# A routed feed-forward kernel: the second layer's third tile in Strassen's form on two column halves

## The chip, the core and the metric

The kernel runs on one core of one Trainium2 chip. The metric is the device time of one execution in microseconds. The core's engines run side by side, each from its own instruction queue: TensorE (PE in the profile, its weight loads PEld) multiplies matrices, VectorE (DVE) and ScalarE (ACT) work element by element, GpSimd (POOL) does so too and here also issues the indirect transfers (gathers and scatters), SyncE (SP) issues plain transfers.

## What is computed

Attention with a decay, block by block, then a layer that sends each token to one of eight experts:

```python
for b in range(nb):                         # 12 blocks of 64 positions, 4 batches, 8 heads of 64
    intra = einsum('bhic,bhjc->bhij', qb, kb) * Dmask
    out[:, :, sl] = einsum('bhij,bhjd->bhid', intra, vb) + einsum('bhid,bhde->bhie', qb * lam_pow, kv_state)
    kv_state = lam_block * kv_state + einsum('bhsd,bhse->bhde', kb * rev_pow, vb)

logits = x @ w_gate                         # x: 3072 tokens of 512
expert_idx = argmax(logits, axis=1)
gate_w = probs[arange(N), expert_idx]       # softmax of the logits
for e in range(8):
    h = maximum(x[mask] @ w1[e], 0.0)       # 512 -> 1024
    out[mask] = gate_w[mask, None] * (h @ w2[e])   # 1024 -> 512
```

All of it is in fp32.

## The kernel before

Everything is written for a scheduler that works from priorities: the program's order gives each instruction its rank, the pools give buffers, and the scheduler fixes one order for each engine's queue and puts in the semaphores. An engine then takes its own queue strictly in that order. Some instructions are pinned to the written order (`keep_in_program_order`).

The attention comes first (to about 125 us in the profile). It leaves every token's row in a table in memory (`xs`) and writes each token into a list of its expert. After it come nine passes over the experts. Passes `0a` and `0b` are the first expert in two parts, multiplied in the plain way (`hidden`, `outputs`). The other seven experts are sorted by their number of tokens, and each is one pass with 424, 408, 408, 384, 368, 368 and 360 places (the "fast" passes). A pass has tiles of 128 places; with 424 or 408 places there is a fourth one of 40 or 24.

Each fast pass multiplies with Strassen's method in Winograd's form. A product of two by two blocks is built from seven products instead of eight, of sums of the blocks of the left side (s1 to s4) and of the right (t1 to t4). `form` (L481) gives the seven products and their additions, `left_sums` (L495) and `right_sums` (L502) the sums before them.

- First layer, `hidden_fast` (L540): the left side is the first weight matrix, its sums made by GpSimd (`first_sums`, tiles `s_q`, `s_k`, `s_v`, and one in place in `w1t`), the right side the tokens, turned so that features lie on the partitions (`xgT`), their sums by VectorE (`token_sums`). The loop runs over two chunks of four of the eight feature chunks: seven products a chunk, each of four matmuls (L549) of 128x128 weights by half the places. Products take three PSUM banks in turn (`ph_banks`); a product can begin once the product three before it has been read out by VectorE or ScalarE. The sums land in `hT`, and ScalarE applies the relu (L560).
- Second layer, `outputs_fast` (L570): `pair_sums` (L562) has VectorE make the sums of tiles 0 and 1 of `hT` in four operations of 512 columns (tiles `h_qsT`, `h_qT`, `h_kT`, `h_kd`). Then tile 2, and tile 3 where there is one, are multiplied in the plain way by `outputs` (L596): eight matmuls (L608) of a tile's `hT` by 512 columns of the second weights `w2t`. A tile of at most 64 (or 32) places is spread over two (or four) groups of the array's columns, with the eight matmuls taking the groups in turn, and the partial results are added afterwards. Then the pair of tiles 0 and 1 by `form` (seven products of four matmuls, L577, 128x128 by 256), with sums of `w2t` that GpSimd made (`second_sums`, tiles `t_q`, `t_k`, `t_v`, `t_m`). Each result is multiplied by the token's gate and scattered to its row (L440). Products take banks 7, 4 and 5 in turn.
- Between them, for the next pass: `turn` (L458) transposes the gathered rows (L463) into two PSUM banks, from which VectorE and ScalarE copy them into `xgT` (L450, L448). `fetch` (L426) gathers the rows of the pass after that; it waits until the transposes have released the gather's buffer.

GpSimd's sums are one instruction of 1024 columns each (L510, L513), eight a pass. The sums of the first weights and those of the second share three tags of one pool (`q`, `k`, `v`, three buffers each), so each waits for an earlier one's last reader.

The order of a fast pass on TensorE, as it is in the profile: first layer; transposes of the next pass, with one matmul of tile 2 (two records) between their two halves; the rest of tile 2; tile 3; the pair. The last pass has no transposes.

Of the kernel before, what the change touches and what calls it, by code (L numbers as in the profile page):

```python
# [10 lines left out]
F32 = mybir.dt.float32  # L11
I32 = mybir.dt.int32
AX = mybir.AxisListType
ALU = mybir.AluOpType
ACT = mybir.ActivationFunctionType
# [5 lines left out]
def kernel(  # L21
# [459 lines left out]
    def form(product, sums_of, temps, give):  # L481

        a, b = sums_of
        p1, u2, u3, u4 = temps
        nc.scalar.copy(p1, product(a.a11, b.b11))
        nc.vector.tensor_add(u2, product(a.s2, b.t2), p1)
        nc.vector.tensor_add(u3, product(a.s3, b.t3), u2)
        p5 = product(a.s1, b.t1)
        give(1, 1, p5, u3)
        nc.vector.tensor_add(u4, p5, u2)  # L490
        give(0, 0, product(a.a12, b.b21), p1)
        give(0, 1, product(a.s4, b.b22), u4)
        give(1, 0, product(a.a22, b.t4), u3)

    def left_sums(a, s1, s2, s3, s4, sub, add):  # L495
        sub(s3, a[0][0], a[1][0])  # L496
        add(s1, a[1][0], a[1][1])
        sub(s2, s1, a[0][0])
        sub(s4, a[0][1], s2)
        return SimpleNamespace(a11=a[0][0], a12=a[0][1], a22=a[1][1], s1=s1, s2=s2, s3=s3, s4=s4)  # L500

    def right_sums(b, t1, t2, t3, t4, sub):  # L502
# [3 lines left out]
        sub(t4, b[1][0], t2)  # L506
        return SimpleNamespace(b11=b[0][0], b21=b[1][0], b22=b[1][1], t1=t1, t2=t2, t3=t3, t4=t4)

    def pool_add(o, x, y):
        return nc.gpsimd.tensor_tensor(out=o, in0=x, in1=y, op=ALU.add)  # L510

    def pool_sub(o, x, y):
        return nc.gpsimd.tensor_tensor(out=o, in0=x, in1=y, op=ALU.subtract)  # L513

    def pool_sub_last(o, x, y):

        tc.keep_in_program_order(pool_sub(o, x, y))

    def first_sums(w1t):
        a = [[w1t[:, j * DH:(j + 1) * DH, i * FH:(i + 1) * FH] for j in range(2)] for i in range(2)]  # L520
# [17 lines left out]
        m.b = right_sums(b, t1, t2, b[0][1], t4, nc.vector.tensor_sub)  # L538

    def hidden_fast(m, w):  # L540
        m.hT = ffn.tile([P, FC, m.n], F32, tag="hT", name="hT", bufs=1)
        h = m.n // 2

        for c in range(0, FC // 2, 2):
            def product(lhs, rhs):
                p = bank(next(ph_banks), [P, 2, h], "p")
                for i in range(2):
                    for dc in range(DH):
                        nc.tensor.matmul(p[:, i, :], lhsT=lhs[:, dc, (c + i) * P:(c + i + 1) * P],  # L549
                                         rhs=rhs[:, dc, :], start=(dc == 0), stop=(dc == DH - 1))  # L550
                return p

            outs = [[m.hT[:, i * FC // 2 + c:i * FC // 2 + c + 2, k * h:(k + 1) * h]
                     for k in range(2)] for i in range(2)]
            temps = [work.tile([P, 2, h], F32, tag=t, name=f"u_{t}", bufs=n)
                     for t, n in (("qT", 2), ("kT", 2), ("qsT", 4), ("kd", 2))]
            form(product, (w, m.b), temps,
                 lambda i, k, p, u: nc.vector.tensor_add(outs[i][k], p, u))  # L558
            for i, k in ((1, 1), (0, 0), (0, 1), (1, 0)):
                nc.scalar.activation(outs[i][k], outs[i][k], ACT.Relu)  # L560

    def pair_sums(m):  # L562

        a = [[m.hT[:, j * FC // 2:(j + 1) * FC // 2, i * P:(i + 1) * P] for j in range(2)]
             for i in range(2)]
        sums = [work.tile([P, FC // 2, P], F32, tag=t, name=f"h_{t}", bufs=n)
                for t, n in (("qT", 2), ("kT", 2), ("qsT", 4), ("kd", 2))]
        return left_sums(a, *sums, nc.vector.tensor_sub, nc.vector.tensor_add)

    def outputs_fast(m, w2t, w2):  # L570
        a = pair_sums(m)
        outputs(m, w2t, range(2, len(m.widths)))

        def product(lhs, rhs):
            p = bank(next(po_banks), [P, MD // 2], "p")
            for fc in range(FC // 2):
                nc.tensor.matmul(p, lhsT=lhs[:, fc, :], rhs=rhs[:, fc, :],  # L577
                                 start=(fc == 0), stop=(fc == FC // 2 - 1))
            return p

        o = [ffn.tile([P, MD], F32, tag="o", name="o", bufs=4) for i in range(2)]
        outs = [[o[i][:, k * MD // 2:(k + 1) * MD // 2] for k in range(2)] for i in range(2)]
        two = [work.tile([P, 2, MD // 2], F32, tag="x", name="u", bufs=3) for i in range(2)]
        temps = [two[i][:, k, :] for i in range(2) for k in range(2)]

        def give(i, k, p, u):
            gate = at(m, i)[2]
            nc.scalar.activation(outs[i][k], u, ACT.Copy, scale=gate)
            nc.vector.scalar_tensor_tensor(out=outs[i][k], in0=p, scalar=gate, in1=outs[i][k],  # L589
                                           op0=ALU.mult, op1=ALU.add)  # L590

        form(product, (a, w2), temps, give)
        for i in range(2):
            scatter(at(m, i)[1], o[i])

    def outputs(m, w2t, tiles=None):  # L596
        for t in tiles or range(len(m.widths)):
            w = m.widths[t]


# [250 lines left out]
```

## Time and profile before

Fourteen runs took 471.04 to 475.26 us, the median is 472.95 us. One execution was profiled: it took 472.61 us, and its span from the first to the last instruction is 470.8 us. Engines are counted busy by their instructions; matmuls are pipelined and their ends are modelled, so their rows overlap, and the steps between the starts say how long one holds the array.

| stretch of the profiled execution (us) | length | PE busy | DVE busy | ACT busy | POOL busy |
|---|---|---|---|---|---|
| 161.4 to 182.0, pass 0b | 20.60 | 20.60 | 6.06 | 3.38 | 12.06 |
| 182.0 to 227.7, pass with 424 places | 45.70 | 45.70 | 20.07 | 9.93 | 38.09 |
| 227.7 to 270.7, 408 | 43.00 | 43.00 | 19.60 | 9.10 | 25.59 |
| 270.7 to 312.5, 408 | 41.80 | 41.80 | 19.39 | 9.06 | 25.58 |
| 312.5 to 351.0, 384 | 38.50 | 38.50 | 16.68 | 8.20 | 24.44 |
| 351.0 to 388.9, 368 | 37.90 | 37.90 | 16.47 | 8.09 | 25.31 |
| 388.9 to 427.9, 368 | 39.00 | 37.91 | 20.70 | 8.12 | 20.21 |
| 427.9 to 470.8, 360 and the end | 42.90 | 36.02 | 14.30 | 7.13 | 4.11 |
| whole execution: 472.61 us, span | 470.8 | 452.3 | 222.4 | 125.8 | 247.7 |

A row of the profile gives an instruction's line, its engine, what it writes from what (out<-in), the shapes, how long it took, and, in brackets, how long its engine stood idle before it and what ended that wait. An fp32 matmul leaves two records on PE and two weight loads on PEld.

### The profile page before, as it was taken

How to read it: one execution, taken by the hardware profiler on the slowest of the kernel's cores; microseconds unless marked ns; L12 is line 12 of the kernel's file. 1: busy time of each engine (PE TensorE's matmuls, PEld its weight loads, DVE VectorE, ACT ScalarE, POOL GpSimd, SP SyncE). 2: the span in 40 equal slices, each digit the busy share in tenths (PEclk: the TensorE clock that was granted, in tenths of full speed). 3: DMA queues.
4: the chain of work that ended last, by engine and by line, in shares of the span. 5: the costliest groups of instructions: out<-in, count | busy, mean ns of one | idle time of the engine just before them, and what ended most of it. 6: DMA issues, size and time to landing. Idle time of an engine off the chain costs nothing.

```text
span 470.8 us, 8695 instructions
## 1 busy us (share of the span) xinstructions
PE 452.3 (96%) x3468; PEld 377.4 (80%) x3468; DVE 222.4 (47%) x525; ACT 125.8 (27%) x323; POOL 247.7 (53%) x189
## 2 busy tenths in 40 slices
PE   4899999999999999999999999999999999999994
PEld 3799999998786576956994898699699689779863
DVE  2657658486450133452345436424524623753421
ACT  3364454554320111222131222013112212211210
POOL 4423745514333939949806951992695497711001
PEclk9999999999999999999999999999999999999998
DMA  9999999999417656160506152451624516001001
GB/s 166 234 252 265 217 244 213 233 307 294 135 47 254 197 197 251 58 249 30 205 19 246 39 213 80 164 186 64 244 78 168 218 43 225 0 20 45 1 17 52
DMA packets 99856, 72.60 MB, mean 154 GB/s; under 512 B 81251, under 2 KB 81255, under 8 KB 99808
## 3 DMA queue, kind: packets, MB, share of 16 engines
q1 hardware_dynamic: 88688, 51.97, 39.8%
q0 software_dynamic: 5008, 13.16, 7.9%
q10 hardware_dynamic: 6112, 6.83, 4.4%
q8 instruction: 29, 0.48, 0.4%
q14 instruction: 19, 0.16, 0.1%
HBM read 58.88 MB, written 13.16 MB: 153 GB/s over the span
## 4 chain that ended last, share of the span: by engine, by line
PE 70%; issue 3%; DVE 1%; DMA 1%; POOL 0%; POOLq 0%; ACT 0%
PE p L549 27%; PE p L577 18%; PE po L608 17%; PE ph L473 5%; PE tp L463 3%; DMA xg<-xs,list_0a 1%; DVE h_qsT L496 0%; PE tx L324 0%; DVE hT L558 0%; POOL slots L388 0%; PE tx L326 0%; DVE xgT L450 0%; PE rank L375 0%; POOLq L804 0%; ACT hT L560 0%
## 5 line engine op out<-in xcount | busy, mean ns | idle before, releaser
L608 PE MATMUL po<-w2t,hT 128*128 128x512 f32 (+5 forms) x224 | 81.0, 596 | 0.0
L434 POOL DMA_INDIRECT xg<-xs,list x24 | 25.9, 1078 | 70.9 <-PE tp L463 65.4
L608 PEld LDWEIGHTS po<-w2t,hT 128*128 128x128 f32 (+5 forms) x224 | 30.5, 161 | 38.2 <-issue 37.9
L560 ACT ACTIVATE hT<-hT 128x408 f32<-128x408 f32 (+4 forms) x56 | 29.5, 527 | 86.7 <-DVE hT L558 86.7
L440 POOL DMA_INDIRECT out_dram<-o,list x24 | 23.9, 994 | 50.9 <-DVE o L614 27.7
L388 POOL DMA_INDIRECT slots<-entry,slot_i x24 | 23.6, 985 | 34.8 <-DVE slot_i L386 13.6
L549 PE MATMUL p<-xgT,w1t 128*128 128x204 f32 (+4 forms) x224 | 41.5, 328 | 0.0
L549 PEld LDWEIGHTS p<-xgT,w1t 128*128 128x128 f32 x224 | 37.6, 190 | 1.2 <-issue 0.9
L236 POOL TENSOR_TENSOR kd<-k_in,kdec 128x512 f32<-128x512 f32 x20 | 20.4, 1043 | 26.4 <-PE cp L299 14.6
L252 DVE TENSOR_TENSOR mt<-sp,decay 128x512 f32<-128x512 f32 x48 | 29.8, 682 | 7.1 <-PE sp L246 7.1
L589 DVE SCALAR_TENSOR_TENSOR o<-p,list,o 128x256 f32<-128x256 f32 x28 | 13.6, 484 | 32.9 <-PE p L577 17.0
L577 PE MATMUL p<-w2t,hT 128*128 128x256 f32 x112 | 26.8, 382 | 0.0
L577 PEld LDWEIGHTS p<-w2t,hT 128*128 128x128 f32 x112 | 21.0, 190 | 7.0 <-issue 4.5
L246 PE MATMUL sp<-qT,kT 64*128 64x128 f32 x384 | 25.6, 285 | 0.0
L246 PEld LDWEIGHTS sp<-qT,kT 64*128 64x128 f32 x384 | 23.3, 194 | 2.2 <-issue 1.9
L282 PE MATMUL op<-mt,v_in 128*64 128x128 f32 x384 | 23.6, 274 | 0.4 <-ACT fence L278 0.4
L558 DVE TENSOR_TENSOR hT<-p,u_qsT 128x408 f32<-128x408 f32 (+4 forms) x28 | 15.7, 561 | 15.8 <-PE p L549 15.8
L473 PE MATMUL ph<-xgT,w1t 128*128 128x256 f32 (+1 forms) x128 | 22.6, 332 | 0.0
L211 PE MATMUL tq<-ident,q_in 128*128 128x128 f32 x96 | 15.4, 286 | 7.2 <-DMA q_in<-in_q_dram 7.2
L463 PEld LDWEIGHTS tp<-ident,xg 128*128 128x128 f32 (+3 forms) x112 | 13.3, 140 | 11.2 <-issue 3.6
L291 ACT COPY xT<-op 128x512 f32<-128x512 f32 x24 | 12.9, 589 | 33.4 <-PE op L270 29.6
L282 PEld LDWEIGHTS op<-mt,v_in 128*64 128x64 f32 x384 | 20.7, 137 | 1.2 <-ACT fence L278 0.9
(162 smaller groups left out, 946.3 us busy)
## 6 DMA issues: line engine op xcount, KB each, us to landing
w1t<-in_moe_w_dram SPq DMA_DIRECT2D x8, 2048.0 KB, 8.3
w2t<-in_moe_w_dram SPq DMA_DIRECT2D x8, 2048.0 KB, 8.5
xs<-x ACTq DMA_DIRECT2D x24, 256.0 KB, 5.0
q_in<-in_q_dram SPq DMA_DIRECT2D x11, 512.0 KB, 8.3
k_in<-in_k_dram SPq DMA_DIRECT2D x11, 512.0 KB, 8.0
v_in<-in_v_dram SPq DMA_DIRECT2D x11, 512.0 KB, 8.6
q_in<-in_q_dram SPq DMA_DIRECT2D x2, 256.0 KB, 6.0
k_in<-in_k_dram ACTq DMA_DIRECT2D x2, 256.0 KB, 4.7
```

The lines of the kernel that those rows point to most:

```text
L246: pin(nc.tensor.matmul(sp[u][:, i, b, :], lhsT=m.kT[s][halves[u], i, b, :], rhs=m.qT[s][halves[u], i, b, :], start=(i == 0 and b == 0), st ...
L252: nc.vector.tensor_mul(mt[:, u], sp[u], decay[:, u, s * HP // 2:(s + 1) * HP // 2].unsqueeze(2).to_broadcast(shp))
L282: pin(nc.tensor.matmul(out_at(m, b, u, hp), lhsT=m.v[:, b, 2 * hp + u, :], rhs=m.mt[hp // 2][:, u, hp % 2, b, :], start=(m.n == 0 and hp = ...
L388: put = nc.gpsimd.indirect_dma_start(out=slots, out_offset=bass.IndirectOffsetOnAxis(ap=slot_i[:, i:i + 1], axis=0), in_=entry[:, n, b, :] ...
L434: nc.gpsimd.indirect_dma_start(out=dst, out_offset=None, in_=xs[:rows, :], in_offset=bass.IndirectOffsetOnAxis(ap=idx, axis=0))
L440: put = nc.gpsimd.indirect_dma_start(out=out, out_offset=bass.IndirectOffsetOnAxis(ap=idx, axis=0), in_=src, in_offset=None, bounds_check= ...
L463: pin(nc.tensor.transpose(tp[:, t * P:t * P + w], m.xg[t // 2][:w, t % 2, dc * P:(dc + 1) * P], ident[:w, :w]))
L473: nc.tensor.matmul(ph, lhsT=w1t[:, dc, fc * P:(fc + 1) * P], rhs=m.xgT[:, dc, :], start=(dc == 0), stop=(dc == DC - 1))
L549: nc.tensor.matmul(p[:, i, :], lhsT=lhs[:, dc, (c + i) * P:(c + i + 1) * P], rhs=rhs[:, dc, :], start=(dc == 0), stop=(dc == DH - 1))
L560: nc.scalar.activation(outs[i][k], outs[i][k], ACT.Relu)
L577: nc.tensor.matmul(p, lhsT=lhs[:, fc, :], rhs=rhs[:, fc, :], start=(fc == 0), stop=(fc == FC // 2 - 1))
L608: nc.tensor.matmul(po[part], lhsT=m.hT[:, fc, t * P:t * P + w], rhs=w2t[:, fc, :], start=(i < k), stop=(i >= FC - k), skip_group_check=True)
```

## The change

It touches the fast passes alone.

1. Tile 2 is no longer multiplied by `outputs`; a new function `single_fast` does it after the pair. It takes the tile's 128 places as two halves of 64 and multiplies them in the same form of seven products with the same sums of `w2t`. Two products run at a time, one on the lower 64 columns of the array, the other on the upper 64, their matmuls taking turns: three such double products of eight matmuls of 128x64 by 256, and the seventh product split into two halves of 128 columns. The evacuations are of 64 partitions.
2. The lists of the passes with less than 384 places are padded: `hT` is made 384 wide and VectorE sets its last columns to zero, so that the third tile always has two halves of 64. What is scattered is still the tile's own places.
3. The sums of `hT` for the pair, and those for the third tile, are made within the first layer, after each of its two chunks (`hidden_blocks` lays them out): per chunk four operations of 256 columns and four of 128, in place of four of 512 for the pair at the end.
4. In `form` the product of a12 and b21 comes second instead of fifth, and the relus follow in the new order.
5. GpSimd's sums are issued in pieces of 256 columns: 32 instructions a pass in place of 8.

```diff
     def form(product, sums_of, temps, give):
         nc.scalar.copy(p1, product(a.a11, b.b11))
+        give(0, 0, product(a.a12, b.b21), p1)
         nc.vector.tensor_add(u2, product(a.s2, b.t2), p1)
         nc.vector.tensor_add(u3, product(a.s3, b.t3), u2)
         p5 = product(a.s1, b.t1)
         give(1, 1, p5, u3)
         nc.vector.tensor_add(u4, p5, u2)
-        give(0, 0, product(a.a12, b.b21), p1)
         give(0, 1, product(a.s4, b.b22), u4)
         give(1, 0, product(a.a22, b.t4), u3)
...
+    def pool(op, o, x, y, done=lambda inst: inst):
+        n = o.shape[2]
+        step = min(n, 256)
+        for c, j in itertools.product(range(o.shape[1]), range(0, n, step)):
+            part = (slice(None), c, slice(j, j + step))
+            done(nc.gpsimd.tensor_tensor(out=o[part], in0=x[part], in1=y[part], op=op))
...
     def hidden_fast(m, w):
-        m.hT = ffn.tile([P, FC, m.n], F32, tag="hT", name="hT", bufs=1)
+        m.hT = ffn.tile([P, FC, max(m.n, TG * P)], F32, tag="hT", name="hT", bufs=1)
+        if m.n < TG * P:
+            nc.vector.memset(m.hT[:, :, m.n:], 0.0)
+        m.sums = hidden_blocks(m)
...
-            for i, k in ((1, 1), (0, 0), (0, 1), (1, 0)):
+            for i, k in ((0, 0), (1, 1), (0, 1), (1, 0)):
                 nc.scalar.activation(outs[i][k], outs[i][k], ACT.Relu)
+            for a in m.sums:
+                chunks = [[block[:, c:c + 2] for block in row] for row in a.blocks]
+                left_sums(chunks, *(t[:, c:c + 2] for t in (a.s1, a.s2, a.s3, a.s4)),
+                          nc.vector.tensor_sub, nc.vector.tensor_add)
+
+    def hidden_blocks(m):
+        both = []
+        for t, w in ((0, P), (2, P // 2)):
+            a = [[m.hT[:, j * FC // 2:(j + 1) * FC // 2, t * P + i * w:t * P + (i + 1) * w]
+                  for j in range(2)] for i in range(2)]
+            sums = ([work.tile([P, FC // 2, w], F32, tag=tag, name=f"h_{tag}", bufs=n)
+                     for tag, n in (("qT", 2), ("kT", 2), ("qsT", 4), ("kd", 2))] if t == 0
+                    else [ffn.tile([P, FC // 2, w], F32, name=f"g_{j}", tag=f"g_{j}", bufs=1)
+                          for j in range(4)])
+            both.append(SimpleNamespace(blocks=a, a11=a[0][0], a12=a[0][1], a22=a[1][1],
+                                        **{f"s{j + 1}": t for j, t in enumerate(sums)}))
+        return both
...
     def outputs_fast(m, w2t, w2):
-        a = pair_sums(m)
-        outputs(m, w2t, range(2, len(m.widths)))
+        outputs(m, w2t, range(3, len(m.widths)))
...
-        form(product, (a, w2), temps, give)
+        form(product, (m.sums[0], w2), temps, give)
         for i in range(2):
             scatter(at(m, i)[1], o[i])
+        single_fast(m, m.sums[1], w2)
+
+    def single_fast(m, a, b):
+        lo, hi = slice(0, P // 2), slice(P // 2, P)
+        half = MD // 2
+
+        def two(*products):
+            p = bank(next(po_banks), [P, half], "p2")
+            for fc in range(FC // 2):
+                for part, (lhs, rhs) in zip((lo, hi), products):
+                    nc.tensor.matmul(p[part, :rhs.shape[2]], lhsT=lhs[:, fc, :], rhs=rhs[:, fc, :],
+                                     start=(fc == 0), stop=(fc == FC // 2 - 1),
+                                     skip_group_check=True)
+            return p
...
+        p = two((a.a11, b.b11), (a.a12, b.b21))
+        nc.scalar.copy(p1, p[lo])
+        start(o[lo, :half], lo, p1)
+        add(o[lo, :half], lo, p[hi])
+        p = two((a.s2, b.t2), (a.s3, b.t3))
+        nc.vector.tensor_add(u2, p[lo], p1)
+        nc.vector.tensor_add(u3, p[hi], u2)
+        for k in range(2):
+            start(o[hi, k * half:(k + 1) * half], hi, u3)
+        p = two((a.s1, b.t1), (a.s4, b.b22))
+        nc.vector.tensor_add(u4, p[lo], u2)
+        add(o[hi, half:], hi, p[lo])
+        start(o[lo, half:], lo, u4)
+        add(o[lo, half:], lo, p[hi])
+        p = two((a.a22, b.t4[:, :, :half // 2]), (a.a22, b.t4[:, :, half // 2:]))
+        for k, part in enumerate((lo, hi)):
+            add(o[hi, k * half // 2:(k + 1) * half // 2], hi, p[part, :half // 2])
+        scatter(idx, o[:w])
```

`start` is a ScalarE copy scaled by the gate, `add` a VectorE operation that multiplies by the gate and adds. `pool_add`, `pool_sub` and `pool_sub_last` now call `pool`.

More of the change, by code (lines that the diff above doesn't have):

```diff
@@ L507, in right_sums @@
         return SimpleNamespace(b11=b[0][0], b21=b[1][0], b22=b[1][1], t1=t1, t2=t2, t3=t3, t4=t4)
+    def pool(op, o, x, y, done=lambda inst: inst):
[4 more added lines that the diff above has]
+            done(nc.gpsimd.tensor_tensor(out=o[part], in0=x[part], in1=y[part], op=op))
     def pool_add(o, x, y):
-        return nc.gpsimd.tensor_tensor(out=o, in0=x, in1=y, op=ALU.add)
+        pool(ALU.add, o, x, y)
     def pool_sub(o, x, y):
-        return nc.gpsimd.tensor_tensor(out=o, in0=x, in1=y, op=ALU.subtract)
+        pool(ALU.subtract, o, x, y)
     def pool_sub_last(o, x, y):
-        tc.keep_in_program_order(pool_sub(o, x, y))
+        pool(ALU.subtract, o, x, y, tc.keep_in_program_order)
     def first_sums(w1t):
@@ L558, in hidden_fast @@
                  lambda i, k, p, u: nc.vector.tensor_add(outs[i][k], p, u))
-            for i, k in ((1, 1), (0, 0), (0, 1), (1, 0)):
+            for i, k in ((0, 0), (1, 1), (0, 1), (1, 0)):
                 nc.scalar.activation(outs[i][k], outs[i][k], ACT.Relu)
[L562 to L568, printed above, removed]
+            for a in m.sums:
[14 more added lines that the diff above has]
+        return both
     def outputs_fast(m, w2t, w2):
-        a = pair_sums(m)
-        outputs(m, w2t, range(2, len(m.widths)))
+        outputs(m, w2t, range(3, len(m.widths)))
         def product(lhs, rhs):
@@ L590, in give, with start, add @@
                                            op0=ALU.mult, op1=ALU.add)
-        form(product, (a, w2), temps, give)
+        form(product, (m.sums[0], w2), temps, give)
         for i in range(2):
             scatter(at(m, i)[1], o[i])
+        single_fast(m, m.sums[1], w2)
[10 more added lines that the diff above has]
+            return p
+        w, idx, gate = m.widths[2], at(m, 2)[1], m.list[:, 2, 2:3]
+        o = ffn.tile([P, MD], F32, tag="o", name="o", bufs=4)
+        u = work.tile([P, 2, half], F32, tag="x", name="u3", bufs=3)
+        p1, u2 = u[lo, 0], u[lo, 1]
+        v = work.tile([P, half], F32, tag="xT", name="u4")
+        u3, u4 = v[hi], v[lo]
+        def start(out, part, src):
+            nc.scalar.activation(out, src, ACT.Copy, scale=gate[part])
+        def add(out, part, p):
+            nc.vector.scalar_tensor_tensor(out=out, in0=p, scalar=gate[part], in1=out,
+                                           op0=ALU.mult, op1=ALU.add)
+        p = two((a.a11, b.b11), (a.a12, b.b21))
[16 more added lines that the diff above has]
+        scatter(idx, o[:w])
@@ L596, in outputs @@
     def outputs(m, w2t, tiles=None):
-        for t in tiles or range(len(m.widths)):
+        for t in range(len(m.widths)) if tiles is None else tiles:
             w = m.widths[t]
```

## The prediction

> **What bounds the kernel now.** I read the page's first part, then the chain that ended last, then TensorE's rows where the change touches them, then VectorE beside GpSimd.
>
> ```profile
> PE 452.3 (96%) x3468; PEld 377.4 (80%) x3468; DVE 222.4 (47%) x525; ACT 125.8 (27%) x323; POOL 247.7 (53%) x189
> ```
>
> TensorE is busy for 96% of the span. From 125 us on, the only gaps of its rows above 0.3 us are one of 0.89 us before the experts begin (at 129.1) and one of 1.09 us (at 409.05). The chain shows the order in which an expert's work follows itself:
>
> ```profile
> 182.02 20.27 PE p L549 x112
> 202.29 1.14 PE tp L463 x8
> 203.43 1.05 PE po L608 x2
> 204.48 1.14 PE tp L463 x8
> 205.62 9.77 PE po L608 x30
> 215.39 12.29 PE p L577 x56
> ...
> 444.97 6.87 PE po L608 x16
> 451.83 12.10 PE p L577 x56
> 463.94 0.03 issue
> 463.96 0.49 DVE o L589
> ```
>
> Every fp32 matmul leaves two records. First layer (L549), the next expert's transposes (L463) with one matmul of tile 2 between them, the rest of tiles 2 and 3 (L608), the pair of tiles 0 and 1 (L577): TensorE is the chain, so a microsecond taken from it is a microsecond of the span, and one that it waits is lost. The last expert has tile 2 alone: 6.87 us for 16 records, 0.429 us each. The pair: 12.10 us for 56 records of 256 columns, 0.216 us each. The 1.09 us gap is explained by the next views, GpSimd's and VectorE's timelines at 405 us:
>
> ```profile
> 405.20 2.36 POOL L513 TENSOR_TENSOR t_v<-w2t 128x1024 f32<-128x1024 f32 x1 [2.62 <-PE p L549]
> 407.51 2.80 POOL L513 TENSOR_TENSOR t_k<-w2t,t_q 128x1024 f32<-128x1024 f32 x1
> ```
>
> ```profile
> 406.27 1.84 DVE L496 TENSOR_TENSOR h_qsT<-hT 128x512 f32<-128x512 f32 x1 [0.58 <-ACT hT L560]
> 408.03 0.53 DVE L558 TENSOR_TENSOR hT<-p,u_qsT 128x368 f32<-128x368 f32 x1
> ```
>
> The VectorE sum of two SBUF operands, 0.69 us at 330.54 where GpSimd gathers, takes 1.84 us: it ends about 0.5 us after GpSimd's t_v (405.20 + 2.36 = 407.56). GpSimd's t_k is then longer by 0.45. The add with a PSUM operand at 408.03, inside t_k, is not slowed. So such sums and GpSimd's take turns, whole instructions at a time.
>
> **The third tile (a gain).** Removed per expert: 16 records of 0.429 = 6.86 us. Added: three double products of 16 records, 64 weight columns by 256, and one of 16 records by 128. Do two column halves run at once? The weight loads of the 40-wide tile 3:
>
> ```profile
> 210.81 0.19 PEld L608 LDWEIGHTS po<-w2t,hT 128*128 128x128 f32 x1 [0.24 <-issue]
> 211.76 0.16 PEld L608 LDWEIGHTS po<-w2t,hT 128*40 128x40 f32 x4 [0.76 <-issue]
> 212.22 0.12 PEld L608 LDWEIGHTS po<-w2t,hT 128*40 128x40 f32 x2 [0.30 <-issue]
> ...
> 214.37 0.12 PEld L608 LDWEIGHTS po<-w2t,hT 128*40 128x40 f32 x2 [0.30 <-issue]
> 215.32 0.73 PEld L577 LDWEIGHTS p<-w2t,hT 128*128 128x128 f32 x4 [0.83 <-issue]
> ```
>
> Two loads come every 0.43 us where one did: pairs at full rate. With different right operands too, as the attention's line 282 shows:
>
> ```profile
> L282 PE MATMUL op<-mt,v_in x32: 272/273/275, 66.6 to 68.2; 128*64 128x128 f32 x32
> ```
>
> 32 records of 64 by 128 start within 1.6 us, 0.107 per pair. So 24 pairs x 0.216 + 8 x 0.107 = 6.04 us. The change of width costs: narrow work begins at 211.76 where the last wide record (211.24 + 0.43) ended at 211.67, 0.09; the pair begins at 215.32 where the last narrow ones (214.80 + 0.43) ended at 215.23, 0.09; the first step on each side is longer (211.76 to 212.22 is 0.03 over; on the way out, where the first load is not hidden, 0.1). Together 0.33. Net 6.86 - 6.37 = 0.49 saved; seven experts 3.4, and the last has no way out: **-3.6 us**.
>
> [...]
>
> **Tile 3 in the place of tile 2 (a loss).** In three experts (424, 408, 408 places) tile 3 is now what stands between the transposes. The instruction order of the changed kernel puts 3, 5 and 1 of its eight matmuls there and 5, 3 and 7 behind. Undivided, the 40-wide tile takes four rounds of two groups, the 24-wide two rounds of four, a round being 2 x 0.43. Divided, 3 + 5 make 2 + 3 rounds, 5 + 3 make 2 + 1, 1 + 7 make 1 + 2: one round more each, 3 x 0.86 = 2.57, with some 0.2 for the extra changes of width. **+2.8** (bounds 0, if the holes were filled, and 3.2).
>
> **Sums by chunks (mostly hidden).** From the rows of 512 columns (0.69) and 360 (0.53) a sum of 256 takes 0.43 and one of 128 0.30. VectorE gets 8 + 8 where it had 4 of 0.69: +3.1 us per expert, and 8 evacuations of half height for one. Its 16.5 us of 37.9 (351 to 388.9) leave room; only its order can hurt, in four places.
> At the end of the first layer two small sums of the half tile now stand ahead of the copy that frees a transpose bank; against the 256-wide sum that got shorter by 0.25 that is +0.23. Where one wide step (0.86) is all that covers it (before: copy done at 332.15, second transposes just then), TensorE waits: experts 3, 4, 5 of seven, **+0.75**; behind the longer steps of experts 1 and 2 it costs nothing.
> In the middle of the first layer, the sums of chunk one stand ahead of the add that frees the bank of the second product. Undisturbed they end 2.8 us after the chunk, the add at 3.3, and TensorE needs that bank after four products, 4 x 1.25 = 5.0: hidden. But in the first fast expert GpSimd runs its weight sums from 179.0 to past 199, and chunk one ends at 182.0 + 10.1. Then seven sums each wait for one GpSimd piece: 0.85 + 7 x 0.63 + 2.05 + 0.55 = 7.9 us, against 4 x 1.45 = 5.8: **+2.0** (0 to 3).
> In experts 5 and 6 GpSimd's sums now start after the third tile's second double product frees t_k and end about when chunk one does: one or two pieces, 1.2 us, inside the 1.7 spare; nothing, at most 1 each.
> In the sixth expert (409.05) three waits of one piece stand where one wait of 1.2 us stood: the copy comes at the same 2.8 us after the layer: 0, give or take 0.5.
>
> **GpSimd's pieces.** A quarter of 2.36 is 0.59 without a fixed part. GpSimd copies of 128 and 64 columns take 0.282 and 0.226, so a fixed part is at most 0.17, the piece 0.72. Sums follow each other at 2.31 to 2.44, almost gapless, so I take 0.63. Per expert 32 pieces are 20.2 us for 18.9, and GpSimd stands idle for 5 to 16 us before each expert's first gather (65.4 us in all, for the transposes). Only one gather has no such slack: the two issued behind the first weight sums (165.2, 166.5) land at 169.9, the transposes need the last at 170.85. 16 pieces are later by 0.5 (up to 2.0): **+0.3** (0 to 1.1). The padding's memset of 16 or 24 columns of 8 rows hides under the 2.5 us before VectorE's next add.
>
> **Queues.** On GpSimd the third tile's scatter now follows the next weight sums, with a whole expert until its buffer is wanted again. On SP the load of the second weights waits for the third double product, 0.9 us before the expert's end, where it was issued 1.6 before (349.45 of 351.05); it takes 8.5 us to land and GpSimd reads it over 20 us after its issue (349.45 to 375.15). ScalarE gets five short copies more per expert and drops one of tile 2's at most; it is 27% busy. These three I cost at nothing; without that slack each would delay GpSimd's sums, which have an expert's time to spare (375.15 to 427.9 for one pair's).
>
> **The end.** Before, one operation (0.49) follows the last matmul. Now VectorE's queue has two adds of 128 columns (0.36 each, from 0.484 at 256 and 0.746 at 512) with one of 256 between that waited for ScalarE: 1.25 us after the last matmul. **+0.75** (0.3 to 0.9). The scatter after it is the same.
>
> **Sum**: -3.6 + 2.8 + 0.75 + 2.0 + 0.3 + 0.75 = +3.0. The profiled execution took 472.61 us with a span of 470.8; the median of the runs is 472.95, 0.34 above it. 470.8 + 3.0 = 473.8 as span, **475.9 us** as median.
>
> **Rivals.**
> A, only the rounds and the end cost: GpSimd's pieces let VectorE through and every sum hides: -3.6 + 2.8 + 0.3 = -0.5, 472.5 us. For it: the pieces are short, and VectorE is idle half the time. Against: at 405 us turns are strict.
> B, faster: tile 3's matmuls lose no round, since TensorE holds eight narrow ones ready or the transposes fill the holes, and the waits hide partly: -3.6 + 0.2 + 0.75 + 1 = -1.7, 471.3 us; all hidden 469.9. Against: matmuls start in the order written, and the transposes use the whole array.
> C, GpSimd decides: pieces at 0.72 end its weight sums some 4 us into chunk one's sums in experts 5 and 6, each then waits 1 us, the first expert 3, the gather 1.1: +3.0 + 2 + 1 + 0.8 = +6.8, 479.8 us. It decides from a piece of about 0.68 us on. Against: gapless rows.
> D, the halves don't overlap: 12.1 us for 6.0 per expert, +42, 518 us. Against: line 282.
>
> **How the numbers follow.** Chances: forecast 0.58, A 0.17, B 0.14, C 0.10, D 0.01. About 0.2% (0.95 us) is what a measurement can tell from none. Faster than 472.0: most of B, 0.14; within: A and the low edge of the forecast, 0.19; slower 0.67. The range 471.4 to 479.0 leaves out half of B, the far half of C and D; the forecast's own is 474.0 to 478.0.
>
> **What would show it.** Third tile: double products at 1.72 us and 0.87, 6.3 to 6.4 per expert; a product of 3 would end the forecast. Rounds: narrow tile 3 in five or three rounds of 0.86, not four or two. First fast expert: a TensorE gap near 198 us with VectorE sums of 0.9 to 1.1 us beside GpSimd. GpSimd's piece near 0.63. Transposes of experts 3 to 5 late by 0.25. One last VectorE row 1.25 us after the last matmul. The prediction is wrong if the first layer of the first fast expert stays at 20.3 us, or if tile 3 keeps its 3.8 and 2.0 us.

## The result and the profile after

The changed kernel takes 490.39 us, the median of ten runs (489.34 to 494.64), beside 472.54 us for the kernel before on the same chips: 1.0381 of it, 95% interval 1.0359 to 1.0402. It is slower, as forecast, but by 17.9 us where 3.0 were forecast, far outside the range. The profiled execution took 491.98 us with a span of 489.9.

The page's first, second and fourth part, of the changed kernel: busy time of each engine, the granted TensorE clock in 40 slices, and the shares of the chain that ended last.

```profile
PE 455.5 (93%) x3804; PEld 389.5 (80%) x3804; DVE 271.8 (55%) x661; ACT 142.0 (29%) x358; POOL 271.8 (55%) x357
...
PEclk9899999999999999999999999599999999999997
...
PE 63%; DVE 7%; issue 4%; DMA 1%; POOL 0%; ACT 0%; POOLq 0%; DVEq 0%
```

TensorE has only 3 us more to do, but its share falls from 96% to 93%, and VectorE's share of the chain rises from 1% to 7%. One slice of the clock, the 26th, reads 5. That slice lies in one expert. The length of each fast expert, from TensorE's first record of its first layer to that of the next expert (the last to the end of the span), worked out from TensorE's rows of each profile:

| kernel | 424 | 408 | 408 | 384 | 368 | 368 | 360, end | sum |
|---|---|---|---|---|---|---|---|---|
| before | 45.56 | 42.99 | 41.78 | 38.60 | 37.85 | 38.98 | 43.04 | 288.80 |
| changed | 46.98 | 43.26 | **56.05** | 38.16 | 37.42 | 39.33 | 43.59 | 304.78 |
| tile 3 behind the pair (e5) | 45.89 | 42.33 | 41.14 | 38.16 | 37.42 | 39.32 | 43.51 | 287.77 |
| the same, GpSimd waiting (e4) | 45.90 | 42.34 | 41.14 | 38.33 | 37.45 | 37.49 | 43.76 | 286.41 |
| fastest (e10) | 44.69 | 42.34 | 41.14 | 38.16 | 37.53 | 37.55 | 42.83 | 284.24 |
| fastest, third tile plain (e12) | 45.56 | 42.99 | 41.63 | 38.45 | 37.71 | 37.70 | 42.63 | 286.68 |

Of the 16.0 us between the first two rows, 14.3 lie in the third expert. (The other 3.1 us between the two profiles lie before the fast experts, in work that the change leaves alone; the profiles of the first five experiments reach the fast experts 1.1 us earlier to 1.1 later than that of before. What they are was not settled. This profiled execution is also 1.6 us above the median of its kernel.)

TensorE's timeline there, changed kernel: start, length, engine, line, operation, tiles, shape; in brackets the idle time before it and who ended it.

```profile
302.68 1.46 PE L598 MATMUL p<-t_v,h_qsT 128*128 128x256 f32 x6
314.87 3.75 PE L598 MATMUL p<-t_k,h_kT 128*128 128x256 f32 x8 [10.73 <-DVE o L685]
318.41 1.06 PE L598 MATMUL p<-t_v,h_qsT 128*128 128x256 f32 x2
319.26 2.54 PE L598 MATMUL p<-t_q,h_qT 128*128 128x256 f32 x8
321.64 1.89 PE L598 MATMUL p<-w2t,h_kd 128*128 128x256 f32 x8
```

In the middle of the pair TensorE stands for 10.73 us. Then eight records, which take 1.89 us in the last line of the fence, take 3.75: the granted clock is 0.50 from 306.91 to 320.56, around the slice that reads 5. From 314.87 to the start of the third tile at 325.18 there are 10.31 us for 34 records that take 34 x 0.2155 = 7.33 at full clock, so the gap costs 3.0 us more: 13.7 in all in this execution. Without it the seven experts are 304.78 - 13.7 - 288.80 = +2.3 us, near the forecast's +3.0.

What the bank waited for is in the timelines of VectorE and GpSimd, changed kernel.

```profile
299.96 0.74 DVE L685 SCALAR_TENSOR_TENSOR o<-po,list,o 24x512 f32<-24x512 f32 x1 [1.07 <-ACT o L681]
300.63 0.54 DVE L504 TENSOR_TENSOR xgT<-xgT 128x384 f32<-128x384 f32 x1
301.10 11.60 DVE L505 TENSOR_TENSOR t_x<-xgT,t_sd 128x384 f32<-128x384 f32 x1
312.73 0.74 DVE L685 SCALAR_TENSOR_TENSOR o<-po,list,o 24x512 f32<-24x512 f32 x1
313.40 0.54 DVE L506 TENSOR_TENSOR t_xT<-xgT,t_x 128x384 f32<-128x384 f32 x1
313.97 0.75 DVE L685 SCALAR_TENSOR_TENSOR o<-po,list,o 24x512 f32<-24x512 f32 x1
```

```profile
300.08 1.26 POOL L434 DMA_INDIRECT xg<-xs,list  x1 [0.30 <-issue]
301.36 2.77 POOL L515 TENSOR_TENSOR t_q<-w2t 128x256 f32<-128x256 f32 x4
304.09 2.75 POOL L515 TENSOR_TENSOR t_v<-w2t 128x256 f32<-128x256 f32 x4
306.81 2.75 POOL L515 TENSOR_TENSOR t_k<-w2t,t_q 128x256 f32<-128x256 f32 x4
309.53 2.75 POOL L515 TENSOR_TENSOR t_m<-w2t,t_k 128x256 f32<-128x256 f32 x4
```

The sum `t_x`, two operands from SBUF, takes 0.52 to 0.59 us throughout the kernel before. Here it begins 0.26 us ahead of GpSimd's `t_q` and ends 0.41 us after the last piece of `t_m`, through all sixteen pieces: 11.60 us. Behind it on VectorE's queue stand the evacuations of tile 3 (L685), whose bank the pair's next product needs. In the kernel before, the last of the tokens' four sums, `t_xT`, ended 0.8 us or more ahead of `t_q`, and `t_x` 1.9 us or more, in every expert but the sixth, where both come behind GpSimd's stream. The third expert of before:

```profile
294.20 0.55 DVE L505 TENSOR_TENSOR t_x<-xgT,t_sd 128x384 f32<-128x384 f32 x1
295.28 0.55 DVE L506 TENSOR_TENSOR t_xT<-xgT,t_x 128x384 f32<-128x384 f32 x1
...
296.67 2.36 POOL L513 TENSOR_TENSOR t_q<-w2t 128x1024 f32<-128x1024 f32 x1
```

What put it later: tile 3, now cut in two among the transposes, finishes sooner, and the first of its evacuations (299.96) is queued ahead of `t_x`; it waited 1.07 us for ScalarE.

The change's other rows, in the chain of the changed kernel (start, length, what):

```profile
206.69 1.14 PE tp L463 x8
207.83 1.84 PE po L677 x6
209.67 1.29 PE tp L463 x8
210.96 2.70 PE po L677 x10
213.66 12.29 PE p L598 x56
225.94 6.20 PE p L627 x64
```

Tile 3 (L677) stands divided between the transposes, and the third tile's double products (L627) take 6.20 us. In the fourth and fifth expert, which have no tile 3, the change does what it was made for: they are 0.44 and 0.43 us shorter (table above).

### The profile page after: what moved, and what is told of

Read it like the earlier page. It is cut to its first block, busy times and chain, and to the rows that moved or that the text cites. A ratio compares the mean times of both kernels' runs of the same rounds, so it can differ in the third digit from the quotient of the medians.

```text
span 489.9 us, 9704 instructions
## 1 busy us (share of the span) xinstructions
PE 455.5 (93%) x3804; PEld 389.5 (80%) x3804; DVE 271.8 (55%) x661; ACT 142.0 (29%) x358; POOL 271.8 (55%) x357
## 4 chain that ended last, share of the span: by engine, by line
PE 63%; DVE 7%; issue 4%; DMA 1%; POOL 0%; ACT 0%; POOLq 0%; DVEq 0%
PE p L561 25%; PE p L598 16%; PE p L627 8%; PE po L677 7%; PE ph L473 4%; PE tp L463 3%; DVE t_x L505 3%; DMA xg<-xs,list_0a 1%; DVE hT L570 1%; DVE o L685 0%; DVE h_kT L498 0%; DVE g L497 0%; DVE g L499 0%; DVE g L498 0%; DVE xgT L504 0%
## 5 line engine op out<-in xcount | busy, mean ns | idle before, releaser
L434 POOL DMA_INDIRECT xg<-xs,list x24 | 24.9, 1037 | 57.3 <-PE tp L463 51.8
L561 PE MATMUL p<-xgT,w1t 128*128 128x204 f32 (+4 forms) x224 | 39.8, 331 | 0.0
L677 PE MATMUL po<-w2t,hT 128*128 128x512 f32 (+3 forms) x112 | 33.7, 597 | 0.0
L609 ACT ACTIVATE o<-u,list 128x256 f32<-128x256 f32 x28 | 13.5, 504 | 57.1 <-DVE u L488 47.9
L598 PE MATMUL p<-t_k,h_kT 128*128 128x256 f32 x56 | 15.1, 418 | 10.7 <-DVE o L685 10.7
L643 DVE SCALAR_TENSOR_TENSOR o<-p,list,o 64x256 f32<-64x256 f32 (+1 forms) x35 | 14.6, 431 | 17.1 <-ACT o L640 16.7
L677 PEld LDWEIGHTS po<-w2t,hT 128*128 128x128 f32 (+3 forms) x112 | 11.3, 140 | 15.2 <-issue 14.6
```

The costliest lines, as they stand in the source:

```text
L434: nc.gpsimd.indirect_dma_start(out=dst, out_offset=None, in_=xs[:rows, :], in_offset=bass.IndirectOffsetOnAxis(ap=idx, axis=0))
L598: nc.tensor.matmul(p, lhsT=lhs[:, fc, :], rhs=rhs[:, fc, :], start=(fc == 0), stop=(fc == FC // 2 - 1))
L677: nc.tensor.matmul(po[part], lhsT=m.hT[:, fc, t * P:t * P + w], rhs=w2t[:, fc, :], start=(i < k), stop=(i >= FC - k), skip_group_check=True)
```

## The experiments

Twelve kernels. "Theory S" in the first expectations is: the pieces are to blame. "M", the author's guess after the first four runs, from `t_x` in the changed kernel (11.60 us) and in e1 (7.62 us, let in at a break of 0.08), is: a VectorE sum with two SBUF operands that stands at the head of a stream of GpSimd sums gets in only at a break in the stream. The last four ran on two chips; on that of e9, e10 and e11 the kernel before took 480.99 us, so that these are read by their ratios.

| run | us, median | ratio to the kernel before, 95% |
|---|---|---|
| e1 changed, whole GpSimd sums | 491.78 | 1.0407 (1.0359 to 1.0456) |
| e2 before, GpSimd sums in pieces | 470.71 | 0.9984 (0.9964 to 1.0004) |
| e3 changed, GpSimd waits for the tokens' sums | 473.23 | 1.0031 (1.0007 to 1.0055) |
| e4 e3 with tile 3 behind the pair | 470.17 | 0.9978 (0.9957 to 0.9999) |
| e5 changed, tile 3 behind the pair | 471.28 | 1.0000 (0.9989 to 1.0012) |
| e6 before, `t_x` made late | 506.66 | 1.0745 (1.0723 to 1.0766) |
| e7 changed, a memset after each sum | 490.10 | 1.0403 (1.0377 to 1.0428) |
| e8 e4 with whole GpSimd sums | 473.68 | 1.0039 (1.0018 to 1.0060) |
| e9 changed, a drain after each sum | 494.39 | 1.028, one run; a second took 504.86 |
| e10 e4, first expert and end rearranged | 476.44 | 0.9907 (0.9872 to 0.9942) |
| e11 e4 with the third tile plain | 487.84 | 1.0139 (1.0098 to 1.0181) |
| e12 e10 with the third tile plain | 469.91 | 0.9981 (0.9964 to 0.9998) |

**e1 and e2: are the pieces to blame?**

```diff
# e1, on the changed kernel
-        n = o.shape[2]
-        step = min(n, 256)
-        for c, j in itertools.product(range(o.shape[1]), range(0, n, step)):
-            part = (slice(None), c, slice(j, j + step))
-            done(nc.gpsimd.tensor_tensor(out=o[part], in0=x[part], in1=y[part], op=op))
+        done(nc.gpsimd.tensor_tensor(out=o, in0=x, in1=y, op=op))
# e2: the kernel before, with the function pool of the changed kernel
```

> The changed kernel with GpSimd's sums whole again (8 instructions of 1024 columns a pass). In the changed kernel one VectorE sum of two SBUF operands (t_x of the third fast pass) lasts 11.6 us, through all sixteen pieces of GpSimd's second-layer sums; TensorE stands for 10.7 us and then runs some 3 us at the lower clock. Theory S (a stream of short GpSimd pieces keeps VectorE's sum out for as long as it lasts, whole sums let it in after one): no VectorE sum lasts over 2.9 us, the 10.7 us gap shrinks to under 2; but in the first and the sixth fast pass each sum may now wait for 2.36 us, some 3 and 2 us more of gap; 479 to 485 us. Theory R (the sum waits for the end of GpSimd's work for another reason, such as a buffer): the gap stays near 10, 488 to 492 us.

> The kernel before with only GpSimd's sums in pieces of 256 columns. Theory S: the pieces cost GpSimd 0.68 us each where a quarter was 0.59, which its idle time holds, and no VectorE sum of two SBUF operands begins just ahead of a stream, since these sums end before the stream begins; so within 1 us of before, 471.5 to 473.5 us, and the gap at 409 us stays between 0.3 and 2. If pieces shut VectorE out wherever the two meet, the sixth fast pass, where they do, loses up to 8 us: 478 to 481 us.

e1 missed: the wait stays. `t_x` begins at 301.17, `t_q` at 301.43, and `t_x` takes 7.62 us, through three whole sums that follow each other without a break; it gets in before the fourth, where GpSimd's rows leave 0.08 us free. TensorE's gap is 8.13 us. The time lies in theory R's range, but R does not fit either: `t_x` ends at 308.79, while GpSimd works on to 310.99. With e2 within its noise of the kernel before, theory S fell: the pieces alone cost nothing, and the shut-out does not need them.

**e3, e4, e5: what takes the wait away?**

```diff
# e3, on the changed kernel
+            seen = small.tile([P, 1], F32, tag="seen", name="seen")
+            tc.keep_in_program_order(nc.gpsimd.tensor_copy(seen, passes[i + 1].b.t4[:, 0, :1]))
             w2_next = second_sums(weights[i][1])
# e4: e3 and this; e5: this alone
     def outputs_fast(m, w2t, w2):
-        outputs(m, w2t, range(3, len(m.widths)))
...
             scatter(at(m, i)[1], o[i])
+        outputs(m, w2t, range(3, len(m.widths)))
         single_fast(m, m.sums[1], w2)
```

The copy of one column reads the last of the tokens' sums, so GpSimd's stream cannot begin before it is done.

> The changed kernel, and GpSimd begins its second-layer sums only after VectorE's last token sum (a copy of one column of it goes ahead of them in GpSimd's queue). Theory S: no sum of two SBUF operands lies beside that stream any more: the 10.7 us gap and the 3 us of lower clock go, and of the 1.6 us of gaps in the sixth fast pass most: 474.5 to 477 us. Theory R: the long VectorE sum stays, 488 to 492 us.

> As the run before this one, and tile 3 is multiplied undivided between the pair and the third tile. If dividing tile 3 among the transposes costs a round of two steps of 0.43 us in each of three passes and the extra changes of width about 0.3 each, as the prediction has it: 3 to 3.6 us less than the run before, 471 to 474 us. If the division was free, the same as the run before.

> The changed kernel, with tile 3's matmuls, evacuations and scatter put behind the pair of tiles 0 and 1, and nothing else (GpSimd does not wait for the tokens' sums). Theory M (the 11.6 us came from the order of VectorE's queue: tile 3's evacuations stood ahead of the sum t_x and pushed its start to 0.26 us before GpSimd's t_q; a sum that stands at the head of such a stream gets in only where GpSimd's queue has a break): t_x ends before t_q begins in every expert, takes 0.53 to 0.58 us, no gap of TensorE above 1.5 us, 470 to 472.5 us, as the kernel that also waits. Rival R2 (GpSimd's stream must be held back, moving tile 3 is not enough): a t_x of over 3 us stays, 480 us or more.

In all three the long `t_x` is gone. e5 lies in its range; e3 and e4 came out 1.3 and 0.8 us below theirs. Holding back GpSimd removes 17 us. Moving tile 3, which takes its evacuations out of the way of `t_x` and leaves the tile undivided, removes 19. Timeline of e5, VectorE and GpSimd:

```profile
293.47 0.55 DVE L505 TENSOR_TENSOR t_x<-xgT,t_sd 128x384 f32<-128x384 f32 x1
294.06 0.61 DVE L506 TENSOR_TENSOR t_xT<-xgT,t_x 128x384 f32<-128x384 f32 x1
...
295.05 2.78 POOL L515 TENSOR_TENSOR t_q<-w2t 128x256 f32<-128x256 f32 x4
```

`t_x` again ends 1.0 us ahead of `t_q` and takes 0.55 us; `t_xT` ends 0.4 us ahead, a thin margin. e4 against e3 also measures the division of tile 3: 3.06 us by the medians, 3.15 in the three experts by the two profiles. What GpSimd's wait adds when tile 3 is out of the way (e5 to e4, 1.1 us) lies in the sixth expert: the gaps of 0.78 and 0.83 us that it has in e5 are not there in e4.

**e6: can the kernel before be made to do it?** Here nothing of the change is in; the sum `t_sd` is only computed again, three to six times.

```diff
# on the kernel before; late is 3, 4, 5, 6 in the third to sixth expert with weight sums, else 0 (the second to fifth fast expert)
+        for _ in range(late):
+            tc.keep_in_program_order(nc.vector.tensor_sub(t1, b[0][1], b[0][0]))
         m.b = right_sums(b, t1, t2, b[0][1], t4, nc.vector.tensor_sub)
```

> The kernel before, whole GpSimd sums and tile 3 as it was, with VectorE's sum t_sd computed three, four, five and six times more in the third to sixth expert with tokens in lists of 408, 384, 368 and 368 (0.47 us each, the result is the same), so that t_x comes later against GpSimd's t_q. By the rows of before t_x would start 1.3, 0.6 and 0.15 us before t_q and 0.3 us inside it. Theory M: with three more nothing happens (0.57 us each); with four t_xT, with five t_x stands before GpSimd's stream begins and is shut out until a break in GpSimd's queue, through two to four whole sums, 5 to 9.5 us; in the sixth the sum that comes inside the first whole sum waits for one or more; TensorE waits for the banks behind them; 477 to 490 us. Theory T (they take turns at the end of each GpSimd sum, and the 11.6 us have to do with the pieces or with something else in the changed kernel): no VectorE sum above 3 us, TensorE waits at most 2 us, 471 to 475 us.

506.66 us, worse than M's 477 to 490: all four experts were hit, also the one meant as a control (the scheduler put the sums of `hT` among the repeats, which made them later than worked out). Timelines of VectorE and GpSimd in the second of them:

```profile
302.86 1.14 DVE L539 TENSOR_TENSOR t_sd<-xgT 128x384 f32<-128x384 f32 x2
303.03 1.19 POOL L434 DMA_INDIRECT xg<-xs,list  x1 [0.30 <-issue]
304.03 7.59 DVE L503 TENSOR_TENSOR t_sd<-xgT 128x384 f32<-128x384 f32 x1
304.24 2.36 POOL L513 TENSOR_TENSOR t_q<-w2t 128x1024 f32<-128x1024 f32 x1
306.54 2.36 POOL L513 TENSOR_TENSOR t_v<-w2t 128x1024 f32<-128x1024 f32 x1
308.85 2.34 POOL L513 TENSOR_TENSOR t_k<-w2t,t_q 128x1024 f32<-128x1024 f32 x1
311.27 2.55 POOL L513 TENSOR_TENSOR t_m<-w2t,t_k 128x1024 f32<-128x1024 f32 x1
311.73 2.51 DVE L504 TENSOR_TENSOR xgT<-xgT 128x384 f32<-128x384 f32 x1
```

Whichever sum of VectorE was under way when `t_q` began was caught, here `t_sd`. 308.85 + 2.34 = 311.19 and the next sum begins at 311.27: at this break of 0.08 us it gets in, ending at 311.62. The sum does not make the break: in the kernel before, with no VectorE sum near, `t_m` begins 0.08 us behind `t_k` in five experts too, and `t_v` and `t_k` follow without one. The next sum then waits for the one GpSimd sum that follows and takes 2.51 us. In the four experts the caught sum began 0.21 to 0.28 us ahead of `t_q` and took 7.59 to 7.68 us; TensorE stood for 5.35, 6.04, 6.69 and 6.81 us. M was right in kind: in e6 the shut-out came with neither the pieces nor anything else of the changed kernel, only from where VectorE's queue stood when GpSimd's stream began. A sum that begins as far ahead of a gather's end, with no GpSimd sum behind the gather, is not held (changed kernel: `t_x` 0.26 to 0.28 us ahead, 0.53 to 0.58 us long).

**e7 and e9: what makes a break?**

```diff
         pool(ALU.subtract, o, x, y, tc.keep_in_program_order)
+        dot = small.tile([P, 1], F32, tag="dot", name="dot")      # e7
+        tc.keep_in_program_order(nc.gpsimd.memset(dot, 0.0))      # e7
+        tc.keep_in_program_order(nc.gpsimd.drain())               # e9
```

> The changed kernel with one GpSimd memset of one column after each of the four sums of the second weights (t_q, t_v, t_k, t_m), so after every fourth piece. Theory M in the form that any instruction of GpSimd's that reads no two operands from SBUF makes a break: t_x, met at the same place, ends behind t_q's four pieces, 2.8 to 3.6 us for 11.6; TensorE's gap falls from 10.7 to 0 to 5 us, 476 to 486 us. Rival M2 (only a stretch in which GpSimd runs nothing lets VectorE in): t_x stays above 9 us, 489 to 493 us.

> The changed kernel with a drain of GpSimd after each of the four sums of the second weights (after t_q, t_v, t_k, t_m). The runs so far: a shut-out sum got in where GpSimd's rows had a break of 0.08 us, and did not where they followed each other without one, a memset of 0.09 us between them included. Theory M (a break admits it): the drain leaves a break of 0.03 to 0.3 us behind t_q's four pieces, and t_x ends there, 2.9 to 3.6 us for 11.6; TensorE's gap at t_k falls from 10.7 to 0 to 5 us; 476 to 486 us. Rival (the breaks were a coincidence; it gets in at the third or fourth sum or when the stream ends): t_x stays above 7 us, 486 to 493 us.

e7 went to the rival: `t_x` takes 11.70 us, TensorE's gap is 10.83. The memsets of 0.09 to 0.10 us lie without a break between the sums, and let nothing in. e9, VectorE and GpSimd:

```profile
308.33 3.45 DVE L505 TENSOR_TENSOR t_x<-xgT,t_sd 128x384 f32<-128x384 f32 x1
308.59 2.77 POOL L515 TENSOR_TENSOR t_q<-w2t 128x256 f32<-128x256 f32 x4
311.81 0.74 DVE L686 SCALAR_TENSOR_TENSOR o<-po,list,o 24x512 f32<-24x512 f32 x1
312.49 0.54 DVE L506 TENSOR_TENSOR t_xT<-xgT,t_x 128x384 f32<-128x384 f32 x1
312.60 3.06 POOL L515 TENSOR_TENSOR t_v<-w2t 128x256 f32<-128x256 f32 x4 [1.24 <-issue]
```

Met at the same place (0.26 us ahead of `t_q`), `t_x` gets in behind `t_q` and takes 3.45 us for 11.60; TensorE's gap falls from 10.73 to 2.59. So in e6, e9 and, unplanned, e1 a stretch in which GpSimd ran nothing (0.08, 1.24 and 0.08 us) admitted VectorE. As a whole e9 took 494.39 us; at 1.028 of the kernel before that would be some 485 on a chip where that takes 471, inside its 476 to 486, but this one run and a second of 504.86 settle nothing. The profile says more: the third expert is 8.8 us shorter than in the changed kernel (47.26 for 56.05), but the break behind `t_q` is 1.24 us, more than thought, and other experts have new gaps of TensorE of 2.13, 1.75 and 1.40 us, so that the seven together gain only 1.5 us (303.29 for 304.78). Draining is no remedy.

**e8: are the pieces worth anything?** e4 with e1's edit.

> The kernel that ran at 470.17 us (tile 3 behind the pair, GpSimd waiting for the tokens' sums), with whole GpSimd sums of 1024 columns in place of pieces. If the pieces are what keeps the sums by chunks cheap in the first fast expert and the sixth (there the changed kernel with whole sums had gaps of TensorE of 3.19 and 2.80 us where pieces had 0.98 and 0.78): 2 to 5 us slower, 472 to 475 us. If the pieces are worth nothing once t_x no longer meets the stream: 469.5 to 471 us.

They are: 473.68 against 470.17 us. TensorE's timeline in the first fast expert of e8:

```profile
196.99 1.60 PE L557 MATMUL p<-xgT,s_k 128*128 128x212 f32 x8
201.77 3.19 PE L557 MATMUL p<-t_sd,w1t 128*128 128x212 f32 x8 [3.19 <-DVE hT L566]
204.76 3.04 PE L557 MATMUL p<-xgT,s_v 128*128 128x212 f32 x8
207.58 1.70 PE L557 MATMUL p<-t_xT,w1t 128*128 128x212 f32 x8
```

Three sums of chunk one, each held up by a whole GpSimd sum, take 1.93 to 2.52 us, the bank is 3.19 us late (0.99 with pieces), and the next 16 records take twice their time (3.19 and 3.04 us for eight, where eight took 1.60 just before); the granted clock is 0.50 from 200.97 to 207.79, and 0.93 as a mean over this expert. This execution took 476.80 us, the longest of ten, at a mean granted clock of 0.985; the two shortest took 471.24 and 471.49 at 0.995. What the clock added thus differed between executions.

**e10 and e12, e11: the terms of the sum.**

```diff
# e10, on e4
-            hidden_fast(m, w1)
+            hidden_fast(m, w1, chunks=(i > 2))       # first fast expert: all sums after the last chunk
...
     def outputs_fast(m, w2t, w2, end):
+        if end:                                      # last expert: third tile ahead of the pair
+            single_fast(m, m.sums[1], w2)
...
-        single_fast(m, m.sums[1], w2)
+        if not end:
+            single_fast(m, m.sums[1], w2)
# e12, on e10 (twice); e11, on e4; both without the third tile's feature sums
-            single_fast(m, m.sums[1], w2)
+            outputs(m, w2t, range(2, 3))
```

> The kernel that ran at 470.17 us (tile 3 behind the pair, GpSimd waiting for the tokens' sums) with two edits: in the first fast expert the feature sums are made whole, behind the last chunk, where GpSimd's weight sums have ended; in the last expert the third tile goes ahead of the pair, so that one VectorE operation follows the last matmul and not three. If the terms of the sum are right: the gap of 0.99 us of the first fast expert goes, the end gets 0.75 to 1.1 us shorter, the third tile gets a second change of width in the last expert, +0.2: 1.5 to 1.9 us less, 468.2 to 468.8 us. If the gap only moves (the whole sums hold up the copy that frees the transposes' bank) or the end is set by something else: 469.3 to 470.5 us.

> The kernel that ran at 470.17 us with the third tile computed plainly, 16 records of 512 columns, at the same place behind tile 3, and no feature sums for it. Isolates the first term of the sum: the prediction's 0.49 us per expert in six experts, 0.82 in the last, less the 0.75 that three VectorE operations cost at the end. In the last expert the plain tile now ends with one evacuation of 512 columns, 0.7 us. By those numbers 2.9 to 3.8 us slower: 473.1 to 474.0 us. If Strassen's form of one tile saves nothing (the changes of width, the extra sums on VectorE): 469.7 to 471 us.

> The fastest kernel so far (tile 3 behind the pair, GpSimd waiting for the tokens' sums, the first fast expert's feature sums whole, the last expert's third tile ahead of the pair; 0.9907 of the kernel before) with the third tile computed plainly and no feature sums for it. The run with the plain third tile before this one did not isolate the term, since a sum by chunks stood 8.33 us in its first fast expert; here those sums are made when GpSimd's stream has ended. The other experts of that run were 0.20 to 0.65 us longer than with Strassen's form. If the first term of the sum is right in kind: 0.2 to 0.65 us per expert more in six, 0.3 to 0.6 in the last, no gap of TensorE above 1 us, 1.5 to 4 us slower than the fastest, 0.994 to 0.999 of the kernel before. If the term is nothing: 0.990 to 0.992.

e10 is the fastest: 0.9907 of the kernel before. TensorE has no gap above 0.4 us in the fast experts; against e4 the first expert is 1.2 us shorter (45.90 to 44.69) and the last, with the end, 0.9 (43.76 to 42.83): 2.2 us over all seven, where 1.5 to 1.9 were expected. Its chain at the end:

```profile
448.79 6.21 PE p L631 x64
455.00 12.30 PE p L600 x56
467.30 0.02 issue
467.32 0.50 DVE o L612
```

One VectorE operation follows the last matmul, where the changed kernel has a row of four adds of 1.64 us in all, mostly after it.

e11 did not measure what it was meant to. VectorE and GpSimd in its first fast expert:

```profile
202.46 0.73 POOL L515 TENSOR_TENSOR s_k<-w1t 128x256 f32<-128x256 f32 x1
202.62 8.33 DVE L497 TENSOR_TENSOR h_qT<-hT 128x256 f32<-128x256 f32 x1 [0.62 <-ACT hT L572]
203.14 2.76 POOL L515 TENSOR_TENSOR w1t<-w1t 128x256 f32<-128x256 f32 x4
205.87 2.76 POOL L515 TENSOR_TENSOR s_q<-w1t 128x256 f32<-128x256 f32 x4
208.60 2.93 POOL L515 TENSOR_TENSOR s_v<-w1t,s_q 128x256 f32<-128x256 f32 x4
```

Without the small sums ahead of it, `h_qT` is shut out too, for 8.33 us, and it had begun 0.16 us after a piece did, not before one. It got in ahead of the last piece, where there is no break. In the changed kernel the sums of the same chunk took turns with the same pieces (196.68 to 201.55, 0.70 to 0.94 us each). So M is too narrow: a break admitted the waiting sum in every meeting of these runs, but between pieces without a break VectorE was let in at once (the sums of 0.70 to 0.94 us), after two or three pieces (changed kernel at 415.87 us, 1.65 us long), after twelve (here, 8.33), or not at all in sixteen (`t_x`, 11.60). What decides that is open; these runs do not tell.

e12 isolates the third tile, with no such meeting: 0.9981 against 0.9907, intervals apart. By the table Strassen's form saves 0.87, 0.65, 0.49, 0.29, 0.18 and 0.15 us in the first six experts and gives back 0.20 in the last with its end: 2.4 us in all by the profiles, 3.5 by the ratios, which come from two chips. The last expert missed its 0.3 to 0.6 us of saving: TensorE's time there falls by 0.36 us (36.20 to 35.83), but what follows the last matmul, the scatters above all, took 0.57 us more in e10's profile, on the other chip.

## Why the prediction was wrong

**The step that failed** is "So such sums and GpSimd's take turns, whole instructions at a time", read from one wait of 1.84 us at 405 us. Turns were seen, but nothing in that view bounds the wait to one instruction: `t_x` was passed by sixteen, e6's sums by three whole ones with nothing of the change in the kernel, e11's by twelve pieces. Rival C, the one in which GpSimd decides, had the right resource and the same bound, one piece for each sum, and so the wrong size; the range took its upper end from there.

**The place was missed as well.** The prediction went through four places where VectorE's order could hurt, all of them feature sums. It moved tile 3's matmuls among the transposes and counted their rounds, but not their evacuations, which move with them in VectorE's queue, ahead of `t_x`. The margin that this used up, 0.8 us from the end of the last tokens' sum to the start of `t_q`, could be read in the trace of before. e5 shows it: tile 3's place alone decides. Then TensorE's clock added 3.0 us to the 10.7.

TensorE slowed after shorter waits as well. After 10.73 us eight records took 3.75 us for 1.89; after 6.04 us in e6 they took 3.75 for 1.89, after 3.19 us in e8 3.19 for 1.60, after 2.59 us in e9 2.94 for 1.89. With waits of 0.98 us in the changed kernel and 1.09 in the kernel before, the granted clock of those experts is 1.00.

The other terms, forecast and measured:

- Third tile, -3.6. The double products take 6.20 to 6.21 us in the changed kernel, and the first layer behind them 0.10 to 0.11 more (17.56 for 17.45 us in the fifth expert): 6.3; forecast 6.04 + 0.33 = 6.37 (the parts of the 0.33 add up to 0.31). Measured by leaving Strassen's form out (e12 against e10), which moves the rows around it as well, the saving is 0.15 to 0.87 us an expert, -2.6 in the first six and -0.4 of TensorE's time in the last (36.20 to 35.83, e12 and e10): -3.0. Right in kind; rival D, halves that do not overlap, is out.
- Tile 3 divided, +2.8: +3.06 (e4 against e3). Right.
- Copies late in the third to fifth expert, +0.75: nothing. The second transposes of these experts take 0.80 to 0.81 us up to TensorE's next work, where they took 0.79 to 0.81.
- First fast expert, +2.0: a gap of 0.98 us at 202.12, 1.2 with what follows (e10). The mechanism is right, seven sums held up by pieces, but they take 5.5 us (196.08 to 201.55) where the forecast had 7 x 0.63 + 2.05 = 6.5.
- First gathers, +0.3: nothing. The transposes that need them begin 9.2 us after the set ahead of them, in the profiles of before and after alike.
- GpSimd's piece, 0.63: 0.71 to 0.72 long and 0.68 from one to the next. At 0.68 and above rival C was to decide, and its 479.8 us would have been nearer; its reason, the pieces' length, was not what decided.
- Sixth expert, 0: +0.35 (gaps of 0.78 and 0.83 for one of 1.09).
- The end, +0.75: +0.9 (e10 against e4), with the third tile's second change of width in it. VectorE's last row ends 1.27 us after the last matmul; 1.25 was worked out.

These come to -3.0 + 3.06 + 1.2 + 0.35 + 0.9 = +2.5, against the +2.3 left in the profile without the shut-out. e3, which removes it, measures +1.5 us (0.3 to 2.6 by its interval); it lacks the sixth expert's gaps too. So the sum was right to about a microsecond, in part by luck: 1.85 us that it added (0.75, 0.3 and 0.8 of the 2.0) did not come, and 1.4 us that it lacked did (0.6 of the third tile, 0.26, 0.35 and 0.15). The direction came out right, but most of the 17.9 us, 13.7 in the profiled execution, came from a wait that it did not have.

## What to carry to other kernels

Where VectorE sums two SBUF operands near a run of back-to-back GpSimd sums, look up the margin between the two in the trace, and treat any edit that uses it up as able to cost the whole run, not one instruction (here `t_x` took 11.60 us for 0.55). When matmuls are moved, follow their evacuations through the queue of the engine that makes them: there they can push a sum of another stage into such a meeting, as tile 3's pushed `t_x` to 0.26 us ahead of `t_q`. The remedy that held was to keep them apart in time (move the evacuations, or let GpSimd wait on the sum); with that, and the two rearrangements of e10, the changed kernel is 0.9% faster than the one before.

## What the hardware showed unexpectedly

- In the changed kernel, e1, e6, e7 and e9 a VectorE sum under way for 0.21 to 0.28 us, about half its time, when a GpSimd stream began had to wait for the end of the stream or a break in it, and then took 0.41 to 0.45 us more, most of its usual 0.53 to 0.58. A GpSimd memset of 0.09 us between sums let nothing in (e7, 11.70 us); 0.08 us without a GpSimd instruction did (e1, 7.62; e6, 7.59).
- Column halves with different right operands run at the full rate: in the third tile two records of 64 by 256 start every 0.215 us, in the pair one of 128 by 256 every 0.216.
- Waits of TensorE of 2.59 us (e9) and 3.19 us (e8) were followed by eight records in 2.94 us for 1.89 and in 3.19 for 1.60; in e8 the granted clock was 0.50 for 6.8 us. With a wait of 1.09 us in the kernel before it was 1.00. In e8's profile a wait of 3.19 us cost about twice its length (the first expert 51.37 us for 45.90 in e4, which has a gap of 0.99).
